# Second-phase weights: lower parts on GpSimd, w_k moved behind a gate, and the last products ordered by bank

## The chip, the cores and the metric

The kernel runs on one core of a Trainium2 chip. The metric is the device time in microseconds (us), the median of several runs, beside one execution that was profiled. Engines are named as in the profile: PE (TensorE, matmul), PEld (its weight load), DVE (VectorE), ACT (ScalarE), POOL (GpSimd), SP (SyncE, which here issues all DMAs).

## What is computed

```python
# attention between x (8 batches, 8 heads, 512 x 64) and a state of 32 rows a head
a   = softmax(x @ state.T / 8);  xread = a  @ state      # 512 rows
a2  = softmax(state @ x.T / 8);  sread = a2 @ x          # 32 rows
x   = concat([xread, sread])                             # 8 x 544 x 512
# first phase
h    = relu(x @ w_in)                                    # 512 -> 1024
conv = conv_w[0]*h[s-1] + conv_w[1]*h[s] + conv_w[2]*h[s+1]
y    = (h * sigmoid(conv)) @ w_out                       # 1024 -> 512
# second phase
prev = y shifted down by one row within a batch
xk = mu_k*y + (1-mu_k)*prev;  xr = mu_r*y + (1-mu_r)*prev
out = sigmoid(xr @ w_r) * (relu(xk @ w_k)**2 @ w_v)
```

Every fp32 operand of a large product is split in two: a high part that the PE's fast fp32 format (float32r) holds, and a low part, the operand less its high part. A product is then three matmuls: high x high, high x low, low x high.

## The kernel before

**Weights.** The weights come as 64-bit numbers. A `Weights` object loads two blocks of 128 x 512 at a time into a staging tile `raw` (line 143, on SP) and splits them: ScalarE makes a scaled copy in `mid` (L161) and converts in place (L163), VectorE puts the bits together in three steps (L164, L165, L166), ScalarE writes the high part (L168), and VectorE subtracts it for the low part (L169). `raw` and `mid` have two buffers each. The first phase uses the same two tags for the tiles `m` in `pair_m`. `weight()` returns the two functions, load and split; `weight_at(w, need, at)` hands both to the half slot `at` with the due number `500 * need - 1000`.

**First phase.** The work goes in slots (batch t, block f of 128 columns of d_ff; eight f a batch; t = 8 is a short one for the 32 state rows of all batches). In a slot `g1_main` makes `hps` on PE from the attention weights and M, the product of state and w_in; ScalarE evacuates it into `hb` (L452), a first tap on ScalarE (L468) and two on VectorE (L470) make the convolution, ScalarE takes the sigmoid (L478), VectorE multiplies (the gate, L479), ScalarE writes the high part of `gs` (L485), and the low part (L487) is made on GpSimd for batches 0 to 2 (`LOW_ON_POOL`), on VectorE later. Two slots on, `g1_sec` multiplies `gs` with w_out into four banks. GpSimd also sets the pads of `hb` (L451) and copies its ends into `carry` (L453). For each pair of batches, `pair_m` makes M in eight groups: ScalarE and VectorE evacuate it (L244, L245), and four DMAs a group copy it into place (L248).

**Second phase.** y goes through DRAM and comes back in nine tiles of tokens (384, seven times 512, 384). `mix` makes `xk` and `xr` for each of four column blocks c: ScalarE (L557), VectorE (L559), the high part on ScalarE (L564), the low part on VectorE (L565). `g2_main` multiplies with w_k, `g2_r` with w_r, and `g2_sec` multiplies the squared result `ks` with w_v into up to four banks; at the last f each bank is multiplied by the sigmoid (L616) and stored (L618).

**Order.** The program is written slot by slot; each piece carries a number (`tc.cur_priority`), and when the program is built a scheduler orders each engine's queue by these numbers and by what it takes to be ready. Space of the attention pool is given back at slot (7, 2), and from there the second phase's weights are announced. The queues run strictly in order. `behind(i)` (line 174) orders instructions traced inside it behind `i` where both are on the same engine's queue; it adds no semaphore.

## Time and profile before

| | |
|---|---|
| median of 3 runs | 883.36 us (883.15 to 884.06) |
| profiled execution | 881.77 us, its span 879.9 us |
| PE busy | 853.5 us, 97% of the span |
| PEld busy | 686.2 us, 78% |
| DVE busy | 546.4 us, 62% |
| ACT busy | 545.6 us, 62% |
| POOL busy | 105.4 us, 12% |

The span is what the trace shows of the profiled execution; the time of that execution is 1.9 us longer. Busy shares are means over the span; a stretch can look quite different. "Granted clock" is the share of full speed that the throttle gave TensorE. A row of the timeline begins with its start in us from the span's start and its duration in us.

### The profile page before, as it was taken

How to read it: one execution, taken by the hardware profiler on the slowest of the kernel's cores; microseconds unless marked ns; L12 is line 12 of the kernel's file. 1: busy time of each engine (PE TensorE's matmuls, PEld its weight loads, DVE VectorE, ACT ScalarE, POOL GpSimd, SP SyncE). 2: the span in 40 equal slices, each digit the busy share in tenths (PEclk: the TensorE clock that was granted, in tenths of full speed). 3: DMA queues.
4: the chain of work that ended last, by engine and by line, in shares of the span. 5: the costliest groups of instructions: out<-in, count | busy, mean ns of one | idle time of the engine just before them, and what ended most of it. 6: DMA issues, size and time to landing. Idle time of an engine off the chain costs nothing.

```text
span 879.9 us, 11844 instructions
## 1 busy us (share of the span) xinstructions
PE 853.5 (97%) x4406; PEld 686.2 (78%) x4406; DVE 546.4 (62%) x908; ACT 545.6 (62%) x952; POOL 105.4 (12%) x215
## 2 busy tenths in 40 slices
PE   5989999999999997999999999999999999999997
PEld 2557787788778775899888888888888888888886
DVE  6899987899799879999645533425334253332311
ACT  6787875787578658888756645636356364553421
POOL 1144543422111111210000000000000000000000
PEclk7899999999999998999999999999999999999999
DMA  9351254525534364233210211011100111001010
GB/s 340 116 197 49 102 143 128 150 75 160 156 114 121 96 197 151 96 144 120 98 48 37 49 48 31 17 48 49 48 23 26 49 48 48 19 18 48 1 48 36
DMA packets 45512, 76.85 MB, mean 87 GB/s; under 512 B 8336, under 2 KB 30352, under 8 KB 43408
## 3 DMA queue, kind: packets, MB, share of 16 engines
q1 hardware_dynamic: 45456, 76.12, 26.6%
q8 instruction: 34, 0.56, 0.3%
q14 instruction: 22, 0.18, 0.1%
HBM read 45.66 MB, written 17.86 MB: 72 GB/s over the span
## 4 chain that ended last, share of the span: by engine, by line
PE 88%; DVE 5%; ACT 3%; DMA 2%; SPq 1%; issue 1%; DVEq 0%; ACTq 0%
PE acc L115 14%; PE acc L116 14%; PE acc L117 14%; PE kps L115 7%; PE kps L116 7%; PE kps L117 7%; PE rps L117 4%; PE rps L116 4%; PE rps L115 4%; PE hps L115 3%; PE hps L117 3%; PE hps L116 3%; PE p_s L297 2%; PE p_m L116 1%; PE p_m L117 1%; SPq L248 1%
## 5 line engine op out<-in xcount | busy, mean ns | idle before, releaser
L594 DVE TENSOR_TENSOR ks<-k,ks 128x512 fp32r<-128x512 f32 (+1 forms) x72 | 47.6, 662 | 119.8 <-ACT ks L593 119.2
L116 PE MATMUL kps<-xk,k 128*128 128x512 f32 (+1 forms) x288 | 110.1, 382 | 0.0
L115 PE MATMUL kps<-xk,k 128*128 128x512 f32 (+1 forms) x288 | 110.1, 383 | 0.0
L117 PE MATMUL kps<-xk,k 128*128 128x512 f32 (+1 forms) x288 | 110.0, 382 | 0.0
L116 PE MATMUL acc<-gs,out 128*128 128x512 f32 (+1 forms) x288 | 109.6, 382 | 0.0
L117 PE MATMUL acc<-gs,out 128*128 128x512 f32 (+1 forms) x288 | 109.1, 380 | 0.0
L115 PE MATMUL acc<-v,ks 128*128 128x512 f32 x272 | 106.7, 392 | 0.0
L116 PE MATMUL acc<-v,ks 128*128 128x512 f32 x272 | 105.9, 389 | 0.0
L117 PE MATMUL acc<-v,ks 128*128 128x512 f32 x272 | 105.8, 392 | 0.0
L470 DVE SCALAR_TENSOR_TENSOR cacc<-hb,vcol,cacc 128x512 f32<-128x512 f32 (+1 forms) x138 | 103.3, 759 | 3.2 <-ACT cacc L468 2.7
L115 PE MATMUL acc<-gs,out 128*128 128x512 f32 (+1 forms) x288 | 95.0, 391 | 5.8 <-ACT gs L485 5.8
L559 DVE SCALAR_TENSOR_TENSOR mix<-yt,muc,mix 128x384 f32<-128x384 f32 (+7 forms) x128 | 61.4, 500 | 47.0 <-ACT mix L557 46.2
L593 ACT ACTIVATE ks<-k 128x512 fp32r<-128x512 f32 (+1 forms) x72 | 43.5, 605 | 71.2 <-PE acc L117 71.0
L557 ACT ACTIVATE mix<-yt,om 128x384 f32<-128x384 f32 (+7 forms) x128 | 61.5, 516 | 33.0 <-DMA yt<-y 16.2
L580 ACT ACTIVATE k<-kps 128x512 f32<-128x512 f32 (+1 forms) x72 | 40.9, 569 | 50.4 <-PE kps L117 50.0
L115 PEld LDWEIGHTS acc<-gs,out 128*128 128x128 f32 x288 | 54.0, 192 | 18.3 <-ACT gs L485 7.3
L116 PEld LDWEIGHTS acc<-gs,out 128*128 128x128 f32 x288 | 54.2, 188 | 13.1 <-issue 2.5
L565 DVE TENSOR_TENSOR xr<-mix,xr 128x512 fp32r<-128x512 f32 (+1 forms) x36 | 23.8, 661 | 62.8 <-ACT xr L564 62.8
L117 PEld LDWEIGHTS acc<-gs,out 128*128 128x128 f32 x288 | 54.2, 188 | 10.6 <-issue 0.8
L116 PEld LDWEIGHTS kps<-xk,k 128*128 128x128 f32 x288 | 54.4, 189 | 10.4
L117 PEld LDWEIGHTS kps<-xk,k 128*128 128x128 f32 x288 | 54.3, 188 | 10.2
L115 PEld LDWEIGHTS kps<-xk,k 128*128 128x128 f32 x288 | 54.2, 188 | 10.2
(138 smaller groups left out, 1762.1 us busy)
## 6 DMA issues: line engine op xcount, KB each, us to landing
out<-r SPq DMA_DIRECT2D x34, 256.0 KB, 2.0
xT<-x_t SPq DMA_DIRECT2D x32, 256.0 KB, 4.0
xn<-x_n SPq DMA_DIRECT2D x8, 1024.0 KB, 4.9
y<-yo SPq DMA_DIRECT2D x8, 1024.0 KB, 4.3
me<-m SPq DMA_DIRECT2D x48, 128.0 KB, 2.4
m_odd<-m SPq DMA_DIRECT2D x48, 128.0 KB, 2.4
raw<-w_out SPq DMA_DIRECT2D x8, 512.0 KB, 4.7
raw<-w_k SPq DMA_DIRECT2D x8, 512.0 KB, 4.5
```

The costliest lines, as they stand in the source:

```text
L115: nc.tensor.matmul(ps, lh, rh, start=start and k == 0, stop=False)
L116: nc.tensor.matmul(ps, lh, rl, start=False, stop=False)
L117: nc.tensor.matmul(ps, ll, rh, start=False, stop=stop and k == last)
L248: nc.sync.dma_start(out=m_of(b + j, q)[ri, :, g].bitcast(F32), in_=r[rj, :, i].bitcast(F32))
L297: nc.tensor.matmul(self.v["s", g][NS * j:NS * (j + 1), :], sT[self.b][r, h // 2, h % 2], xT[self.b][r, h // 2], start=True, stop=True,)
L470: nc.vector.scalar_tensor_tensor(a[:, :n], hb[:, k:k + n], w[k], a[:, :n], op0=ALU.mult, op1=ALU.add)
L557: nc.scalar.activation(tmp[:, o:o + m], y[:, c, q - 1:q - 1 + m], AF.Copy, scale=om[:, i:i + 1])
L559: nc.vector.scalar_tensor_tensor(tmp[:, o:o + m], y[:, c, q:q + m], muc[:, i:i + 1], tmp[:, o:o + m], op0=ALU.mult, op1=ALU.add,)
L565: nc.vector.tensor_tensor(dst[t][:, 1, c, :n], tmp[:, :n], hi.bitcast(F32), op=ALU.subtract)
L580: nc.scalar.activation(k[:, :n], s["p"][:, :n], AF.Relu)
L593: nc.scalar.activation(ks[:, 0, :n], s["k2"][:, :n], AF.Copy)
L594: nc.vector.tensor_tensor(ks[:, 1, :n], s["k2"][:, :n], ks[:, 0, :n].bitcast(F32), op=ALU.subtract)
```

## The change

The low parts of w_k, w_v and w_r are subtracted on GpSimd instead of VectorE (`helper=nc.gpsimd`). The low parts of the first second-phase tile's mixes, xk and xr, are too. The loads of w_k are ordered on SP behind the last copy of M; the ScalarE steps of w_k's splits are ordered behind the sigmoid of batch 7, f = 0, and their VectorE steps behind the gate of the same slot. In the last block of products with w_v, the three matmuls of each bank are ordered behind the last matmul of the bank before.

```diff
--- before.py
+++ after.py
@@ -1,4 +1,4 @@
-from contextlib import ExitStack
+from contextlib import ExitStack, nullcontext
 
 import concourse.bass as bass
 import concourse.tile as tile
@@ -14,6 +14,8 @@
 AX = mybir.AxisListType
 
 LOW_ON_POOL = (0, 1, 2)
+
+MIX_LOW_ON_POOL = (0,)
 
 CONV_ON_PE = 3
 
@@ -114,14 +116,16 @@
         for k, ((lh, ll), (rh, rl)) in enumerate(zip(lhs, rhs)):
             nc.tensor.matmul(ps, lh, rh, start=start and k == 0, stop=False)
             nc.tensor.matmul(ps, lh, rl, start=False, stop=False)
-            nc.tensor.matmul(ps, ll, rh, start=False, stop=stop and k == last)
+            end = nc.tensor.matmul(ps, ll, rh, start=False, stop=stop and k == last)
+        return end
 
 
     class Weights:
 
 
 
-        def __init__(self, src, many, n, pool, tag="", home=None):
+        def __init__(self, src, many, n, pool, tag="", home=None, helper=None):
+            self.helper = helper or nc.vector
             self.src, self.many, self.n, self.pool, self.tag, self.home = src, many, n, pool, tag, home
             self.wide = src[0].dtype != F32
 
@@ -166,7 +170,7 @@
             nc.vector.scalar_tensor_tensor(v, x, 3, v, op0=ALU.logical_shift_left, op1=ALU.bitwise_or)
             return (
                 nc.scalar.activation(hi, vf, AF.Copy),
-                nc.vector.tensor_tensor(lo, vf, hi.bitcast(F32), op=ALU.subtract),
+                self.helper.tensor_tensor(lo, vf, hi.bitcast(F32), op=ALU.subtract),
             )
 
     W = {}
@@ -175,10 +179,23 @@
 
         return tc.issue_after(i.ins)
 
-    def weight(src, key, tag, pool, k, many, group, home=None):
-
-
-        r = Weights([src[k + i] for i in range(many)], many, N, stg, home=home)
+    marks = {}
+
+    def after(fn, *keys):
+
+
+        def run():
+            with ExitStack() as stack:
+                for key in keys:
+                    stack.enter_context(behind(marks[key]))
+                fn()
+
+        return run
+
+    def weight(src, key, tag, pool, k, many, group, **how):
+
+
+        r = Weights([src[k + i] for i in range(many)], many, N, stg, **how)
 
         def split(first=0, n=many):
             g = (key, "group", k // group)
@@ -245,7 +262,9 @@
         nc.vector.tensor_tensor(r[:, 1], src, r[:, 0].bitcast(F32), op=ALU.subtract)
         for j, rj in HALF:
             for i, ri in HALF:
-                nc.sync.dma_start(out=m_of(b + j, q)[ri, :, g].bitcast(F32), in_=r[rj, :, i].bitcast(F32))
+                marks["m"] = nc.sync.dma_start(
+                    out=m_of(b + j, q)[ri, :, g].bitcast(F32), in_=r[rj, :, i].bitcast(F32)
+                )
 
     class Attention:
         def __init__(self, b, ap):
@@ -475,8 +494,8 @@
         n = width(t)
         s = st1[t, f]
         g = s["g"] = cp.tile([P, N], F32, tag="g", name="g")
-        nc.scalar.activation(g[:, :n], s["a"][:, :n], AF.Sigmoid)
-        nc.vector.tensor_tensor(g[:, :n], g[:, :n], s["hb"][:, 1:1 + n], op=ALU.mult)
+        marks["sigmoid", t, f] = nc.scalar.activation(g[:, :n], s["a"][:, :n], AF.Sigmoid)
+        marks["gate", t, f] = nc.vector.tensor_tensor(g[:, :n], g[:, :n], s["hb"][:, 1:1 + n], op=ALU.mult)
 
     def g1_c(t, f):
         n = width(t)
@@ -562,7 +581,8 @@
             )
         hi = dst[t][:, 0, c, :n]
         nc.scalar.activation(hi, tmp[:, :n], AF.Copy)
-        nc.vector.tensor_tensor(dst[t][:, 1, c, :n], tmp[:, :n], hi.bitcast(F32), op=ALU.subtract)
+        eng = nc.gpsimd if t in MIX_LOW_ON_POOL else nc.vector
+        eng.tensor_tensor(dst[t][:, 1, c, :n], tmp[:, :n], hi.bitcast(F32), op=ALU.subtract)
 
     def g2_main(t, f):
         n = W2[t]
@@ -610,7 +630,8 @@
         for i in range(W2[t] // P):
             sl = slice(i * P, (i + 1) * P)
             w = W["v", f]
-            mm3(ps[i], [(ks[:, 0, sl], ks[:, 1, sl])], [(w[:, 0], w[:, 1])], f == 0, f == KF - 1)
+            with behind(end) if i and (t, f) == (NT2 - 1, KF - 1) else nullcontext():
+                end = mm3(ps[i], [(ks[:, 0, sl], ks[:, 1, sl])], [(w[:, 0], w[:, 1])], f == 0, f == KF - 1)
             if f == KF - 1:
                 o = rt[t][:, i]
                 nc.vector.tensor_tensor(o, o, ps[i], op=ALU.mult)
@@ -754,15 +775,16 @@
                 ap_cm.__exit__(None, None, None)
                 p2 = ctx.enter_context(tc.tile_pool(name="p2", bufs=1))
                 for k in range(0, KF, 2):
-                    w = weight(w_k, "k", "wk", p2, k, 2, 2)
+                    w = weight(w_k, "k", "wk", p2, k, 2, 2, helper=nc.gpsimd)
+                    w = after(w[0], "m"), after(w[1], ("sigmoid", B - 1, 0), ("gate", B - 1, 0))
                     h = h2 + 2 * k
                     weight_at(w, h, h - 4)
                 for k in range(0, KF, 2):
-                    w = weight(w_v, "v", "wa", wp, k, 2, 4)
+                    w = weight(w_v, "v", "wa", wp, k, 2, 4, helper=nc.gpsimd)
                     h = h2 + 2 * k + 4
                     weight_at(w, h + 1, h - 3)
                 for k in range(0, KC, 2):
-                    w = weight(w_r, "r", "wb", wp, k, 2, 2)
+                    w = weight(w_r, "r", "wb", wp, k, 2, 2, helper=nc.gpsimd)
                     h = h2 + 8
                     weight_at(w, h, h - 2)
                 at_half(2 * i + 4, lambda: load_y(0, p2))
```

## Rows read from the trace of the kernel before

**Rows 1.** Waits of PE: what it waited for, us in total, times, longest us.

```profile
PE acc L115 <- ACT gs L485: 5.8, 2, 5.6
```

**Rows 2.** Busy time by stretch, six here and that of the twin passage.

```profile
core 0: us, PE busy (x) PEld busy (x) DVE busy (x) ACT busy (x) POOL busy (x), PEclk, DMA share, GB/s
320.00:330.40 10.40, 8.64 (x99) 6.14 (x97) 8.12 (x14) 7.79 (x12) 1.50 (x4) 1.00 0.78 208
...
330.40:335.90 5.50, 0.00 (x0) 0.00 (x0) 4.88 (x8) 5.49 (x8) 0.20 (x2) 0.81 0.99 373
335.90:340.70 4.80, 4.79 (x11) 3.79 (x12) 4.80 (x7) 4.80 (x8) 1.16 (x2) 0.51 0.01 3
...
336.00:417.00 81.00, 81.00 (x439) 72.02 (x440) 79.06 (x123) 69.19 (x121) 12.60 (x33) 0.97 0.30 108
417.00:447.00 30.00, 30.00 (x147) 26.05 (x146) 19.21 (x33) 21.49 (x43) 0.00 (x0) 1.00 0.23 80
...
238.60:249.00 10.40, 10.36 (x111) 7.25 (x110) 7.79 (x15) 9.97 (x17) 0.98 (x7) 1.00 0.69 203
```

**Rows 3.** Timeline of ScalarE at the passage from batch 6 to 7.

```profile
320.06 0.60 ACT L244 ACTIVATE m<-p_m 128x512 fp32r<-128x512 f32 x1 [2.28 <-PE p_m L117]
...
329.08 1.13 ACT L168 ACTIVATE k<-raw 128x1024 fp32r<-128x1024 f32 x1 [0.45 <-PE p_srT L396]
...
333.19 1.12 ACT L161 ACTIVATE mid<-raw 128x1024 f32<-128x1024 f32 x1
334.22 1.12 ACT L163 ACTIVATE raw<-raw 128x1024 uint32<-128x1024 uint32 x1
335.24 0.61 ACT L485 ACTIVATE gs<-g 128x512 fp32r<-128x512 f32 x1
```

**Rows 4.** Timeline of ScalarE at the passage from batch 4 to 5.

```profile
238.67 0.60 ACT L244 ACTIVATE m<-p_m 128x512 fp32r<-128x512 f32 x1 [2.71 <-PE p_m L117]
...
258.58 0.63 ACT L478 ACTIVATE g<-cacc 128x512 f32<-128x512 f32 x1 [0.96 <-DVE cacc L470]
```

**Rows 5.** Timeline of PE at the same passage: the first products with w_out.

```profile
248.13 1.07 PE L115 MATMUL acc<-gs,out 128*128 128x512 f32 x4
```

**Rows 6.** Timeline of the SP queue: four of the weights' loads.

```profile
309.13 1.40 SPq L143 DMA_DIRECT2D raw<-w_k  x2
...
326.69 0.97 SPq L143 DMA_DIRECT2D raw<-w_k  x2
...
360.60 0.80 SPq L143 DMA_DIRECT2D raw<-w_v  x2
384.72 1.94 SPq L143 DMA_DIRECT2D raw<-w_r  x4
```

**Rows 7.** The chain of waits at the end: start, us, what.

```profile
874.59 0.24 PE acc L117
...
874.85 0.69 DVE r L616
875.54 0.60 DVEq L847
876.14 0.60 DVE r L616
```

**Rows 8.** Timeline of VectorE: two gs lows, a weight low and a mix low.

```profile
308.46 1.17 DVE L487 TENSOR_TENSOR gs<-g,gs 128x512 fp32r<-128x512 f32 x1
...
313.53 0.69 DVE L487 TENSOR_TENSOR gs<-g,gs 128x512 fp32r<-128x512 f32 x1
...
343.29 1.21 DVE L169 TENSOR_TENSOR k<-raw,k 128x1024 fp32r<-128x1024 f32 x1
...
368.92 0.55 DVE L565 TENSOR_TENSOR xk<-mix,xk 128x384 fp32r<-128x384 f32 x1
```

**Rows 9.** Timeline of GpSimd: one subtract.

```profile
308.03 1.05 POOL L322 TENSOR_TENSOR q<-q,s 128x512 f32<-128x512 f32 x1 [4.22 <-DVE s L321]
```

**Rows 10.** GpSimd by line and shape: count, busy us, mean ns, idle before.

```profile
L487 POOL TENSOR_TENSOR gs<-g,gs 128x512 fp32r<-128x512 f32 x24 | 35.4, 1476 | 23.4 <-ACT gs L485 23.1
```

**Rows 11.** The conv taps (L470) on VectorE in two stretches: busy us and count.

```profile
100.00:130.00 30.00, 9.80 (x12) 1.00 0.41 112
...
280.00:300.00 20.00, 8.60 (x12) 1.00 0.39 113
```

## The prediction, as written before the result was known

> **What bounds the kernel now.** I read the waits of PE first, because PE is the busy engine: what is worth something is where it stands still. Only one wait of several us lies behind the start-up: 5.6 us before a product of the first phase that needs `gs`, the gated tile that ScalarE writes [rows 1]. Next, the busy time by stretch shows where this is and what the other engines do [rows 2]. From 320.0 to 330.4 PE works 8.64 of 10.4 us, from 330.4 to 335.9 not at all: 1.8 us in pieces and 5.5 in one, 7.3 us in all. The stretch behind it, 335.9 to 340.7, runs at a granted clock of 0.51, that is at 1.2 instead of 2.4 GHz: 4.8 x 0.49 = 2.4 us more. From 336 to 447 PE is never idle. So a change can gain in three places only: this gap, the slow clock behind it, and the end of the kernel. It can lose anywhere behind 336, and there the other columns matter: VectorE is busy 79.06 of 81 us from 336 to 417 and ScalarE 69.19, while 417 to 447 leaves VectorE 10.8 us free.
>
> **What fills the gap.** It lies at the passage from batch 6 to batch 7. ScalarE's queue tells the order of its work [rows 3]: between 329.08 and the `gs` at 335.24 that PE waits for stand a step of w_k's first split (L168, 1.13 us) and two steps of its second (L161 and L163, 1.12 us each), besides a table load and two sigmoids. The same passage from batch 4 to 5 has no second-phase weights in it and serves as a twin [rows 4, 5]: its last M evacuation is at 238.67, against 320.06 here, so the shift is 81.4 us. In the twin PE's product starts at 248.13, with PE busy 10.36 of 10.4 us from 238.6 [rows 2]. Shifted, it would start at 329.5, somewhat earlier even, since the last batch has no next scores to make. Here it starts at 335.9. The difference, 6.4 us or a little more, is most of the 7.3 us of idle time, found by another way.
>
> **Term 1, w_k behind the first gate.** All ScalarE and VectorE steps of the four w_k splits are put behind the sigmoid and the gate of batch 7, f = 0, in their own queues. No semaphore is waited for that was not before; it is an order of queues. At most the gap closes, 7.3 us; at least the three ScalarE steps in it go, 3.4 us. I take 6.8: the twin is the same code with the same queues, and half a microsecond of the pieces before 330.4 may stay, which w_k does not cause. The loads of w_k, eight DMAs in four pairs, are put on SP behind the last copy of M. Before, the first pair stood at 309.13, the second already behind the last copy at 326.69 [rows 6]. The first now goes out late, but the second pair, issued at 326.69, fed an L161 at 333.19, so a load needs at most 6.5 us, and the gate in question comes later than that: the twin's sigmoid of its f = 0 is at 258.58 [rows 4], shifted 340.0, a few us sooner without score work. Behind the loads on SP stand the load of the first y tile and of w_v, both needed tens of us later.
>
> **Term 2, the clock.** The 5.5 us without work are followed by the stretch at half clock. In 320.0 to 330.4, with 1.8 us of idle time in pieces, the granted clock stayed at 1.00 [rows 2]. If only such pieces remain, the 2.4 us come back whole; if 4 us remain in one piece, perhaps nothing does. I take 2.4.
>
> **Term 3, the last block bank by bank.** Before, the nine matmuls of the last f run with the six products of the high part first and the three closing ones last, so three banks close together and VectorE multiplies three times in a row, from 874.85 to 876.74 [rows 7]. Now a bank closes every third matmul: PE ends at the same time, two multiplies run beside it, and one of 0.69 us is left, done at 875.54. That is 1.2 us sooner, and the store behind it is the same. The low part that bank 0's closing product now needs sooner is made by VectorE while PE still works on the f before, so I charge no wait. Bounds 0.6 (one multiply saved) to 1.2.
>
> **Term 4, the lows on GpSimd and the splits moved into a full stretch.** Ten weight lows of 1.21 us and eight mix lows of 0.55 us leave VectorE [rows 8]: 16.5 us. GpSimd has no 1024-wide and no 384-wide subtract in this trace. The nearest rows are 512 wide: 1.05 us for one [rows 9] and 1.48 us on average for the 24 lows of the first batches [rows 10]. By width that gives, as an estimate, 2.1 to 3.0 us for a weight and 0.8 to 1.1 us for a mix, 27 to 38 us in all; up to 417 (seven of each) 20 to 29 us, where GpSimd did 12.6 us of work from 336 on [rows 2]. The two engines hinder each other: while GpSimd subtracted from 308.03 to 309.08, a VectorE subtract begun at 308.46 took 1.17 us; the next of that line took 0.69 [rows 8, 9]. The conv taps of L470 cost 9.80/12 = 0.82 us while the lows of batch 1 ran on GpSimd and 8.60/12 = 0.72 later [rows 11]. Such a slot holds two taps and a gate; with 0.1 us for each tap and somewhat more for the gate I charge 0.38 us of VectorE per low of 1.05 us, that is 36%, or about 10 us for 27. Relief is then 16.5 - 10 = 6.5 us net, between -10.5 us (16.5 against 27) and +16.5 us.
> What comes in: w_k's first split and a part of the second, which had used the gap, now have to fit into the full stretch up to 417. VectorE had 79.06 us of work there; the 81 us shrink to 78.6 with the clock back. Some 3.8 us of splits come in, seven lows of each kind go (12.3 us), and 36% of 20.3 us comes as hindrance (7.3 us): 77.9 us in 78.6. ScalarE goes from 69.2 to about 75. Both are full, so a part of the later splits slips, and there is room behind 417. By need, w_k's first pairs have tens of us in hand; its last pair, w_r and w_v have only a few, and each hands its staging buffer on 1 to 2 us later, since a GpSimd low is longer. Also queued behind a low on GpSimd are the pad memsets of `hb`, which may come 2 to 3 us late. I charge 1.5 us of new PE idle time, between 0 and 5.
>
> The Trainium skill (SBUF — State Buffer, section "Who interferes with whom") calls the port pair that VectorE and GpSimd share an exclusive lock: of a GpSimd instruction that reads SBUF and a VectorE instruction with two SBUF inputs, the one that comes second stands still for the whole of the other. The 1.17 us row agrees with it; the tap means show that VectorE is not caught each time. By the rule, the 16.5 us taken off VectorE could be paid back with 27 us, which is the lower end above and the third rival.
>
> **Sum.** 6.8 + 2.4 + 1.2 - 1.5 = 8.9 us. The profiled execution lasted 881.77 us (its span 879.9 and 1.9 us around it), the median of the runs is 883.36, 1.6 us more; the gain is put against the median: 874.5 us.
>
> **Rivals.**
> First, *another weight takes the place of w_k.* Only w_k is gated. If w_v's first pair took the free staging buffer at 309, its steps L161 to L166 would run in the same gap. Against it: buffers go out in the order of the code, not by due number: w_v's second pair (75,500) was loaded at 360.60, ahead of w_r (75,000) at 384.72 [rows 6]. Its price: only L168 and L169 leave the gap, some 2 us, the clock stays low, and the end gives 1.2: 883.4 - 3 = 880.
> Second, *the gain is given back before 447.* VectorE and ScalarE are so full that the PE time won is waited for at the start of the second phase, where w_k, w_r and the mixes have to be ready 9 us sooner. For it: 79.06 of 81 us. Against it: the room behind 417, and that the first batches had a GpSimd low in each slot and none of PE's long waits. With 9.5 of the 10.4 us given back: 882.5, no change.
> Third, *GpSimd locks VectorE out*, slower than before. If every low up to 417, at its contended length (7 x 3.0 + 7 x 1.1 = 28.7 us), stops VectorE for all of it, against 12.3 us taken off, VectorE has 16.4 us more to do in a stretch with 1.9 us free, and PE waits for some 14 us of it: 883.4 - 10.4 + 14 = 887. It decides from about 10 us of net loss. Against it: the 36% above.
> Fourth, the gap closes fully and nothing is lost behind it: 883.4 - 10.9 = 872.5.
>
> **Chances.** Forecast 0.68 (872.8 to 879), first rival 0.10, second 0.09, third 0.06, fourth 0.07. A measurement of this kernel tells about 0.2% (1.8 us) from no change. Faster: 0.68 + 0.10 + 0.07 = 0.85; within 0.2%: 0.09; slower: 0.06. The range 872.0 to 880.0 takes in the forecast, the fourth case and most of the first.
>
> **What would show it.** In the profile after: no PE wait of microseconds for `gs` near 330, and L161, L163 and L168 of w_k only behind the sigmoid of batch 7, f = 0 (term 1); a granted clock of 1.00 from 330 on (term 2); three multiplies at the end spaced by PE, not back to back (term 3); PE idle time, if any, between 385 and 445, and taps longer than 0.75 us there (term 4). I am wrong if another step fills the gap, or if PE's idle time behind 336 exceeds 5 us.

## The result and the profile after

The changed kernel takes 889.21 us (median of four executions, 889.01 to 891.04) against 883.71 us (883.15 to 884.40) for the kernel before beside it. The ratio is 1.0056, with an interval from 1.0036 to 1.0076: slower by 0.56%, 5.5 us, where 874.5 us had been forecast. The profiled execution of the changed kernel is its slowest, 891.04 us; that of the kernel before, 881.77 us, lies below all four of its executions here, so the two profiles lie further apart than the medians. Up to about 309 us the queues of both kernels hold the same instructions in the same order, and what differs there, some 4 us of PE idle time and clock between 150 and 240, is not of the change; the stretches behind 309 us are what is compared here.

The first lines of the page of the changed kernel give the busy time by engine. VectorE has 18 instructions fewer than before (890 against 908) and is busy 7.6 us longer (546.4 before); GpSimd is busy 37.1 us longer (105.4 before).

```profile
span 889.3 us, 11849 instructions
PE 855.0 (96%) x4406; PEld 685.9 (77%) x4406; DVE 554.0 (62%) x890; ACT 545.5 (61%) x952; POOL 142.5 (16%) x233
```

Next the busy time by stretch (start:end, length, then busy us of PE, PEld, DVE, ACT, POOL with instruction counts, granted clock, DMA share, GB/s), of the kernel before first, then of the changed one. It answers to [rows 2]. PE lost 7.27 us to idle time from 309 to 336 before; it loses 1.54 now, and the clock from 336 to 345 is 1.00 and not 0.74. Behind that PE was never idle before, though VectorE was busy for 58.72 of the 60 us from 345 to 405. Now PE is idle for 9.41 us there, while VectorE works 59.54 us, and the clock falls to 0.94 from 405 to 447.

```profile
309.00:336.00 27.00, 19.73 (x157) 15.69 (x155) 21.46 (x40) 18.73 (x29) 3.15 (x8) 0.96 0.76 243
336.00:345.00 9.00, 9.00 (x30) 7.24 (x31) 9.00 (x12) 8.97 (x14) 1.89 (x4) 0.74 0.01 3
345.00:405.00 60.00, 60.00 (x337) 53.27 (x337) 58.72 (x95) 49.05 (x89) 10.61 (x28) 1.00 0.33 123
```

```profile
309.00:336.00 27.00, 25.46 (x180) 20.27 (x179) 19.93 (x41) 17.63 (x30) 3.69 (x10) 1.00 0.49 151
336.00:345.00 9.00, 9.00 (x42) 7.44 (x40) 9.00 (x15) 7.98 (x12) 1.84 (x5) 1.00 0.43 165
345.00:405.00 60.00, 50.59 (x274) 42.45 (x273) 59.54 (x72) 45.23 (x79) 32.42 (x34) 0.99 0.32 111
405.00:447.00 42.00, 42.00 (x221) 39.26 (x222) 33.71 (x42) 32.14 (x58) 17.36 (x11) 0.94 0.38 131
```

The waits of PE from 336 to 447 name the tiles (what it waited for, us in total, times, longest). All belong to the first phase: `gs`, its low part, an `hb`, and `yo`, the copy of a result bank. No weight of the second phase is among them.

```profile
PE acc L117 <- ACT gs L504: 7.1, 2, 4.5
PE hps L117 <- ACT hb L477: 1.3, 1, 1.3
PE acc L118 <- DVE gs L506: 0.8, 1, 0.8
PE acc L117 <- DVE yo L523: 0.2, 1, 0.2
```

What VectorE and GpSimd do meanwhile is in their timelines (start, duration, line, operation). The first fence is VectorE, the second GpSimd, both of the changed kernel.

```profile
353.35 2.35 DVE L489 SCALAR_TENSOR_TENSOR cacc<-hb,vcol,cacc 128x512 f32<-128x512 f32 x1
356.23 2.31 DVE L489 SCALAR_TENSOR_TENSOR cacc<-hb,vcol,cacc 128x512 f32<-128x512 f32 x1
359.07 0.74 DVE L489 SCALAR_TENSOR_TENSOR cacc<-hb,vcol,cacc 128x512 f32<-128x512 f32 x1
...
400.40 2.65 DVE L489 SCALAR_TENSOR_TENSOR cacc<-hb,vcol,cacc 128x286 f32<-128x286 f32 x1
```

```profile
352.71 2.44 POOL L173 TENSOR_TENSOR k<-raw,k 128x1024 fp32r<-128x1024 f32 x1
...
355.15 2.84 POOL L173 TENSOR_TENSOR k<-raw,k 128x1024 fp32r<-128x1024 f32 x1
...
399.29 3.44 POOL L173 TENSOR_TENSOR v<-raw,v 128x1024 fp32r<-128x1024 f32 x1 [3.67 <-ACT v L172]
```

A tap takes 0.74 us; one that meets a weight low ends about half a us behind that low: the tap of 353.35 at 355.70, the low of 352.71 at 355.15. It goes the other way too: the low of 399.29 begins while VectorE runs a split step (399.26, 1.21 us), and takes 3.44 us. The last of these pairs makes the longest wait of PE, 4.47 us. The next two fences follow it on ScalarE and PE: the sigmoid waits 2.69 us for the tap of 400.40, the `gs` for the gate behind it, and PE 4.47 us for the `gs`. The chain begins with the low of w_v on GpSimd. The second-longest wait, 2.66 us at 363.96, ends differently: the gate of that tile was done at 360.41, but on ScalarE two steps of a w_v split stood ahead of its `gs`, the first of them waiting 0.75 us for its load, and the `gs` began at 363.30.

```profile
403.08 0.44 ACT L497 ACTIVATE g<-cacc 128x286 f32<-128x286 f32 x1 [2.69 <-DVE cacc L489]
404.30 0.44 ACT L504 ACTIVATE gs<-g 128x286 fp32r<-128x286 f32 x1 [0.78 <-DVE g L498]
```

```profile
404.80 1.27 PE L117 MATMUL acc<-gs,out 128*128 128x272 f32 x4 [4.47 <-ACT gs L504]
```

How much VectorE lost shows in its instructions by line and form from 300 to 447 us (busy us, mean ns of one). Of the kernel before first, then of the changed one; the same four forms, whose lines are L470, L479 and L166 before.

```profile
L470 DVE SCALAR_TENSOR_TENSOR cacc<-hb,vcol,cacc 128x512 f32<-128x512 f32 x26 | 19.0, 745 | 0.6 <-ACT cacc L468 0.6
L166 DVE SCALAR_TENSOR_TENSOR raw<-mid,raw 128x1024 uint32<-128x1024 uint32 x10 | 12.2, 1222 | 0.1
L470 DVE SCALAR_TENSOR_TENSOR cacc<-hb,vcol,cacc 128x286 f32<-128x286 f32 x16 | 8.2, 511 | 0.0
L479 DVE TENSOR_TENSOR g<-g,hb 128x286 f32<-128x286 f32 x8 | 3.6, 451 | 0.0
```

```profile
L489 DVE SCALAR_TENSOR_TENSOR cacc<-hb,vcol,cacc 128x512 f32<-128x512 f32 x27 | 23.8, 891 | 0.7 <-ACT cacc L487 0.7
L170 DVE SCALAR_TENSOR_TENSOR raw<-mid,raw 128x1024 uint32<-128x1024 uint32 x10 | 14.4, 1435 | 0.1
L489 DVE SCALAR_TENSOR_TENSOR cacc<-hb,vcol,cacc 128x286 f32<-128x286 f32 x16 | 12.4, 777 | 0.1
L498 DVE TENSOR_TENSOR g<-g,hb 128x286 f32<-128x286 f32 x8 | 6.7, 833 | 0.0
```

And GpSimd's, of the changed kernel: a weight low takes 2.5 to 2.8 us, a mix low 1.4. The 18 lows are 37.9 us.

```profile
L173 POOL TENSOR_TENSOR v<-raw,v 128x1024 fp32r<-128x1024 f32 x4 | 11.1, 2764 | 15.3 <-ACT v L172 15.3
L173 POOL TENSOR_TENSOR k<-raw,k 128x1024 fp32r<-128x1024 f32 x4 | 10.8, 2707 | 0.4 <-ACT k L172 0.4
L585 POOL TENSOR_TENSOR xk<-mix,xk 128x384 fp32r<-128x384 f32 x4 | 5.5, 1376 | 3.5 <-ACT xk L583 3.5
L585 POOL TENSOR_TENSOR xr<-mix,xr 128x384 fp32r<-128x384 f32 x4 | 5.4, 1362 | 0.5 <-ACT xr L583 0.5
L173 POOL TENSOR_TENSOR r<-raw,r 128x1024 fp32r<-128x1024 f32 x2 | 5.1, 2534 | 9.1 <-ACT r L172 9.1
```

The 18 subtracts had been 16.5 us of VectorE. It is busy 7.6 us longer without them, so the rest of its work grew by 24.1 us: 64% of the lows' 37.9 us on GpSimd. The totals of kernels without these lows on GpSimd (before, e1, e4, e16) differ by 1.3 us.

Two of the change's parts did what they were to do. On ScalarE, from M's last evacuation (324.11) w_k's first step waits until 342.05, behind the first sigmoids of batch 7, where before three of w_k's steps stood between 329 and the `gs` that PE waited for [rows 3], and two more ahead of them:

```profile
324.11 0.60 ACT L261 ACTIVATE m<-p_m 128x512 fp32r<-128x512 f32 x1 [2.28 <-PE p_m L119]
...
333.77 0.62 ACT L504 ACTIVATE gs<-g 128x512 fp32r<-128x512 f32 x1
...
342.05 1.14 ACT L165 ACTIVATE mid<-raw 128x1024 f32<-128x1024 f32 x1
```

At the end, the last of the three multiplies is over at 886.27 (one row for three instructions), 0.73 us behind PE's last matmul, which ends at 885.54; before it was 876.73 behind 875.27, 1.46 us [rows 7].

```profile
884.22 2.05 DVE L637 TENSOR_TENSOR r<-r,acc 128x512 f32<-128x512 f32 x3 [3.58 <-PE acc L119]
```

```profile
885.15 0.39 PE L119 MATMUL acc<-v,ks 128*128 128x512 f32 x1
```

### The profile page after: what moved, and what is told of

It reads as the page before. It is cut to its first block, busy times and chain, and to the rows that moved or that the text cites. A ratio compares the mean times of both kernels' runs of the same rounds, so it can differ in the third digit from the quotient of the medians.

```text
span 889.3 us, 11849 instructions
## 1 busy us (share of the span) xinstructions
PE 855.0 (96%) x4406; PEld 685.9 (77%) x4406; DVE 554.0 (62%) x890; ACT 545.5 (61%) x952; POOL 142.5 (16%) x233
## 4 chain that ended last, share of the span: by engine, by line
PE 80%; DVE 11%; ACT 4%; DMA 2%; issue 2%; SPq 1%; ACTq 0%; DVEq 0%
PE acc L117 12%; PE acc L119 12%; PE acc L118 12%; PE kps L117 7%; PE kps L118 7%; PE kps L119 7%; PE rps L119 3%; PE rps L118 3%; PE rps L117 3%; DVE cacc L489 3%; PE hps L117 2%; PE hps L119 2%; PE hps L118 2%; PE p_s L316 2%; DMA me<-m 1%
## 5 line engine op out<-in xcount | busy, mean ns | idle before, releaser
L489 DVE SCALAR_TENSOR_TENSOR cacc<-hb,vcol,cacc 128x512 f32<-128x512 f32 (+1 forms) x138 | 112.3, 824 | 3.4 <-ACT cacc L487 2.7
L578 DVE SCALAR_TENSOR_TENSOR mix<-yt,muc,mix 128x384 f32<-128x384 f32 (+7 forms) x128 | 64.2, 522 | 51.2 <-ACT mix L576 50.2
L118 PEld LDWEIGHTS kps<-xk,k 128*128 128x128 f32 x288 | 54.9, 191 | 10.3
L117 PEld LDWEIGHTS kps<-xk,k 128*128 128x128 f32 x288 | 54.7, 190 | 10.3 <-ACT xk L583 0.2
L119 PEld LDWEIGHTS acc<-gs,out 128*128 128x128 f32 x288 | 54.3, 189 | 10.5 <-issue 0.8
L497 ACT ACTIVATE g<-cacc 128x512 f32<-128x512 f32 (+1 forms) x69 | 41.8, 606 | 30.2 <-DVE cacc L489 19.0
```

Of the source, the lines that this page charges most:

```text
L117: nc.tensor.matmul(ps, lh, rh, start=start and k == 0, stop=False)
L118: nc.tensor.matmul(ps, lh, rl, start=False, stop=False)
L119: end = nc.tensor.matmul(ps, ll, rh, start=False, stop=stop and k == last)
L489: nc.vector.scalar_tensor_tensor(a[:, :n], hb[:, k:k + n], w[k], a[:, :n], op0=ALU.mult, op1=ALU.add)
L497: marks["sigmoid", t, f] = nc.scalar.activation(g[:, :n], s["a"][:, :n], AF.Sigmoid)
L578: nc.vector.scalar_tensor_tensor(tmp[:, o:o + m], y[:, c, q:q + m], muc[:, i:i + 1], tmp[:, o:o + m], op0=ALU.mult, op1=ALU.add,)
```

## The experiments

Two theories stood after the result. **L, the lows**: GpSimd and VectorE stop each other, and that costs more VectorE time than the moved subtracts had been. **F, the full stretch**: from 345 to 405 VectorE has no free time even without that, so what the passage wins is waited for behind it. Two further theories come up in the expectations: **S**, that the chain of the ten splits, which pass through two staging buffers, begins too late; and **Q**, that a split's step holds up ScalarE's queue. All kernels are built from the changed one, and the code cuts are abridged; differences are given against the kernel before in the same session, whose median lay between 883.6 and 884.5 us. Single executions of one kernel differ by 2 to 7 us; in the profiles, waits of PE for the copies of M differ by some us ahead of 309.

### e1, all lows back on VectorE

```diff
-    w = weight(w_k, ..., helper=nc.gpsimd)      # w_v and w_r too
+    w = weight(w_k, ...)
-MIX_LOW_ON_POOL = (0,)
+MIX_LOW_ON_POOL = ()
```

> The change without its GpSimd part: all lows stay on VectorE, w_k behind the gate and the bank order stay. Theory L (the GpSimd lows lock VectorE out of SBUF and that is the whole loss): the gap at the passage 6 to 7 is closed as in the changed kernel, nothing is lost behind it, 873 to 877 us. Rival F (VectorE and ScalarE are too full for the splits once the gap is closed, whoever makes the lows): PE waits of several us between 350 and 420 stay, and VectorE has 16 us more own work, 886 to 893 us.

Measured: 883.49 us (882.02 to 885.53, 12 executions) against 884.38; ratio 0.9983 (0.9968 to 0.9997). It lies between the two expectations, and neither theory alone is right. The lows on GpSimd cost the difference to the changed kernel, some 6 us, but without them the gain of the passage isn't there either. The windows of this kernel show where it went: 309 to 336 is as good as in the changed kernel (1.11 us idle), 336 to 345 runs at 1.00, and PE is idle 5.24 us from 345 to 405, at a clock of 0.97.

```profile
309.00:336.00 27.00, 25.89 (x182) 20.61 (x181) 20.37 (x41) 18.14 (x30) 4.05 (x10) 1.00 0.52 161
336.00:345.00 9.00, 9.00 (x41) 7.48 (x40) 9.00 (x15) 8.35 (x12) 1.49 (x4) 1.00 0.34 132
345.00:405.00 60.00, 54.76 (x296) 47.24 (x296) 59.41 (x92) 50.88 (x88) 18.74 (x26) 0.97 0.34 125
```

The longest of these waits, 2.68 us, shows what stands in the way. The first fence is ScalarE, the second PE. A step of a w_r split waits 1.94 us for its load and the split's next step follows; behind both stands a sigmoid whose last tap had ended at 391.69 at the latest. The gate behind that sigmoid then waits until 395.06 for another step of the split on VectorE. So here it is first ScalarE's queue and then VectorE's.

```profile
391.70 1.16 ACT L165 ACTIVATE mid<-raw 128x1024 f32<-128x1024 f32 x1 [1.94 <-DMA raw<-w_r]
392.76 1.12 ACT L167 ACTIVATE raw<-raw 128x1024 uint32<-128x1024 uint32 x1
393.79 0.42 ACT L497 ACTIVATE g<-cacc 128x286 f32<-128x286 f32 x1
```

```profile
396.10 0.78 PE L117 MATMUL acc<-gs,out 128*128 128x272 f32 x4 [2.68 <-ACT gs L504]
```

### e2, the lows on GpSimd alone

```diff
-    w = after(w[0], "m"), after(w[1], ("sigmoid", B - 1, 0), ("gate", B - 1, 0))
-    with behind(end) if i and (t, f) == (NT2 - 1, KF - 1) else nullcontext():
+    with nullcontext():
```

> The GpSimd part alone: lows of w_k, w_v, w_r and of the first mixes on GpSimd, no gate for w_k, no bank order. Theory L: VectorE instructions of 2 to 3 us appear beside the lows and PE waits between 340 and 420: 8 to 13 us slower than before, 892 to 897 us. Rival F: VectorE is relieved and nothing is squeezed, so 881 to 884 us.

Measured: 894.12 us (893.06 to 897.27, 6); ratio 1.0119 (1.0099 to 1.014), +9.7 us, as theory L expected. The subtracts cost VectorE more on GpSimd than at home (551.2 us busy against 546.4), and this by itself is more than the whole loss of the change.

### e4, the order by bank alone

```diff
-MIX_LOW_ON_POOL = (0,)
+MIX_LOW_ON_POOL = ()
-    helper=nc.gpsimd              # three times
-    w = after(...)                # w_k's loads and splits
```

> The bank order of the last block alone. All theories: the last three multiplies are spaced by PE and the last one ends 1.2 us sooner after PE's last matmul, so 0.6 to 1.2 us less than before, 882.5 to 883.1 us.

Measured: 883.20 us (881.05 to 885.48, 12); ratio 0.9987 (0.9974 to 1.0), -1.2 us with an interval from -2.3 to 0. The traces give the better figure: VectorE ends 0.72 us behind PE in this kernel and 0.73 in the changed one, against 1.46 before.

### e7 and e8, which lows

e7 has the weight lows on GpSimd and the mix lows on VectorE, e8 the reverse.

```diff
-MIX_LOW_ON_POOL = (0,)
+MIX_LOW_ON_POOL = ()         # e7
-    helper=nc.gpsimd          # e8, three times
```

> The changed kernel with the mix lows back on VectorE; only the weight lows are on GpSimd. Theory L: the weights hold some 27 of the 38 us of GpSimd lows, so most of the loss against all lows on VectorE (5.7 us) stays: 886 to 889 us. If the mixes, whose four steps share one buffer, are what hurts: 883 to 885 us.

> The changed kernel with the weight lows back on VectorE; only the first tile's mix lows are on GpSimd. Theory L: 884 to 886 us, against 883.5 with all lows on VectorE. If the mixes are what hurts: 887 to 890 us.

Measured: e7 888.60 us (887.09 to 890.67, 5), ratio 1.0061 (1.0038 to 1.0084); e8 883.96 us (882.22 to 887.05, 10), ratio 1.0002 (0.9987 to 1.0018). The weight lows carry nearly all of it: e7 is within 1 us of the changed kernel, e8 within 1 us of e1.

### e5, each weight low in four pieces

```diff
-    self.helper.tensor_tensor(lo, vf, hi.bitcast(F32), op=ALU.subtract)
+    for j in range(0, self.n, P):
+        s = slice(j, j + P)
+        i = self.helper.tensor_tensor(lo[:, :, s], vf[:, :, s], hi[:, :, s], op=ALU.subtract)
```

> The changed kernel with each weight low cut into four subtracts of 256 columns on GpSimd. Theory L, by sums: VectorE is stopped for 0.5 to 0.9 us at a time instead of 2 to 3, but the port is held as long in all, so 886 to 892 us. Rival S (it is the single long stops that hit the gate and tap chains): VectorE slips in between, 880 to 885 us.

Measured: 889.26 us (888.33 to 890.07, 5); ratio 1.0065 (1.0043 to 1.0086), the time of the changed kernel. So shorter stops brought no time. The 40 pieces of 1.02 to 1.11 us are 41 us on GpSimd, where the ten lows were 27; with the mix lows it is 53 us. VectorE's other work grew by 20.3 us, somewhat less than the 24.1 of the changed kernel, so the sum of VectorE's loss doesn't explain why the time is the same.

The growth per us of lows on GpSimd differs between the kernels: 64% in the changed one, 61% in e2 and e7, 38% here, 32% in e8. GpSimd's own time may be part of the reason, since it grows where VectorE stops it: a mix low takes 2.1 us on the mean in e8 and 1.4 in the changed kernel.

### e6, the lows without their reads

```diff
-    self.helper.tensor_tensor(lo, vf, hi.bitcast(F32), op=ALU.subtract)
+    for j in range(2):
+        self.helper.memset(lo.bitcast(F32), 0.0)
+    self.helper.tensor_tensor(lo[:, :, :1], vf[:, :, :1], hi[:, :, :1], op=ALU.subtract)
+    ...                                           # the mixes' lows likewise
```

> The changed kernel, but each GpSimd low is two fills of the same width and a subtract of one column a block, so GpSimd is busy about as long and hands the tile on as late, yet reads almost nothing; the low parts of these weights and mixes are left out of the result. Theory L (what VectorE loses is the port that GpSimd's reads hold): VectorE's instructions beside them are back at 0.6 to 0.75 us, it is truly relieved of 16 us, and 874 to 880 us result. Rival G (GpSimd is simply slow, so weights, mixes and buffers come late): 887 to 891 us as in the changed kernel.

Measured: 884.75 us (880.43 to 887.29, 10) against 883.99; ratio 0.9999 (0.9977 to 1.0021). It lies between the expectations, and far below the changed kernel: with two fills (2.0 us a weight) in place of each subtract (2.5 to 2.8 us), the 512-wide taps are back at 747 ns, the short ones at 509. The low parts are missing from this kernel's result. One form got longer, the split's `tensor_scalar` with one input (L169; line 176 of this kernel): 994 ns on the mean of ten against 692 before, nearly all in one instance. It lay beside a run of fills from 364.46 to 368.08, and a copy of two columns on GpSimd ended with it.

```profile
365.04 3.58 DVE L176 TENSOR_SCALAR mid<-mid 128x1024 f32<-128x1024 f32 x1
```

So the reads are what VectorE's two-input work meets, and this one step with one input stood still while GpSimd did little but write; PE waited 2.38 us for a low part of `gs` soon after, at 371.07. The fills wait for no result of ScalarE, unlike the subtracts, so the tiles are also handed on sooner here; it is the taps' rows, more than the time, that speak for the reads. The Trainium skill (SBUF — State Buffer, section "Who interferes with whom") says both: a two-input VectorE instruction contends with GpSimd instructions that read SBUF and not with those that only write, and a VectorE instruction in a two-port mode, which `tensor_scalar` can enter, contends with GpSimd, with no such limit to reads. These rows agree, though none names the mode of the step.

### e10 and e12, other places for single splits

Both are e1 with one thing moved. In e10 w_k's first pair is not gated; in e12 w_r's pairs come behind w_k's last.

```diff
+    if k:                                                   # e10
         w = after(w[0], "m"), after(w[1], ("sigmoid", B - 1, 0), ("gate", B - 1, 0))
-    weight_at(w, h, h - 2)                                  # e12
+    weight_at(w, h + 3, h)
```

> The changed kernel with all lows on VectorE, and only the second to fourth pair of w_k behind the first gate; the first pair is loaded and split as before, in the passage's early part. It stands against the kernel with all four pairs gated and the lows on VectorE (883.5). Theory S, what takes the passage's gain back is the late begin of the chain of splits (two staging buffers, ten splits one after the other): the chain begins one pair sooner, and some 4 us of the 8 won stay: 878 to 881. Theory F, it is VectorE, which has no free time from 345 to 405: one split (L168 to L173, about 4 us of VectorE) leaves that stretch and is paid in the passage, where VectorE has some 5 us free in 320 to 345 but its queue then holds back the gs of the passage: 881 to 884, with PE waiting near 330 again.

> The changed kernel with all lows on VectorE, and the two pairs of w_r loaded and split behind the last pair of w_k instead of ahead of it. It stands against 883.5. Theory S: the same ten splits run through the same two buffers, but what ScalarE waits for near 390 (2.6 us in all, a w_r load) is no longer w_r; if the chain's length decides, nothing moves: 882.5 to 884.5; if it was the place of w_r's split ahead of the gated tiles of the last slot of the first phase, the wait near 396 goes, 880 to 882. Theory F: VectorE has the same work in the same stretch: 883 to 885.

Measured: e10 882.85 us (881.33 to 888.21, 11) against 883.61, ratio 0.9999 (0.9982 to 1.0015); e12 883.27 us (881.5 to 885.09, 11), ratio 0.999 (0.9977 to 1.0003). Neither moves the time; theory S had put e10 at 878 to 881. e10 is the plainest picture of a trade: from 345 to 385 PE is never idle, but from 330.4 to 345 it is idle 3.5 us at a clock down to 0.81. One split more in the passage, one less behind it, and the lost time is the same.

### e11, one tap less in batch 7

e1 without one of batch 7's two VectorE taps, 6.1 us less on VectorE in the stretch. The convolution of batch 7 is incomplete in it.

```diff
-    for k in (1, 2):
+    for k in (1, 2)[:1 + (t != B - 1)]:
```

> The changed kernel with all lows on VectorE and one of the two VectorE taps of the convolution of batch 7 left out (so this part of the result is not computed): eight instructions of about 0.76 us, 6.1 us, leave VectorE between 340 and 395, and nothing else changes, the staging of the weights least of all. It stands against 883.5. Theory F, VectorE's full stretch gives the gain back: most of these 6 us come off the end, 877 to 880, and PE's idle time from 345 to 405 shrinks by half or more. Theory S, the chain of staging does: 882 to 884, with the waits of PE near 396 for gs still there.

Measured: 878.68 us (878.07 to 879.75, 5); ratio 0.9946 (0.9933 to 0.9958), -4.9 us, 4 us more than e1 at the middle. This is what theory F expected: relief of VectorE in this stretch comes off the end, two thirds of it. In its windows PE is idle 2.94 us from 345 to 405, at a clock of 1.00, against 5.24 at 0.97 in e1; that is a little less than the half that F had expected. A tap less also makes each tile's way to its gate shorter by about 0.75 us, and this run doesn't tell the two apart.

```profile
345.00:405.00 60.00, 57.06 (x325) 50.05 (x324) 58.02 (x90) 52.28 (x91) 11.40 (x25) 1.00 0.42 155
```

### e13 and e14, the work for r behind the first phase

e13 takes the w_r splits and the mixes for r behind the sixth gate of t = 8, with e12's order; e14 is the same without w_k's gate.

```diff
+    w = w[0], after(w[1], ("sigmoid", B, 5), ("gate", B, 5))            # w_r
-    at_half(h2 + 2 + c, lambda c=c: mix(0, 1, c, p2))
+    at_half(h2 + 2 + c, after(lambda c=c: mix(0, 1, c, p2), ("sigmoid", B, 5), ("gate", B, 5)))
-    if f >= 4 and f - 4 < W2[t] // P:
+    f0 = 4 if t else 5
+    if f >= f0 and f - f0 < W2[t] // P:
```

> All lows on VectorE, w_k behind the first gate and the bank order kept; and what the first phase doesn't need is moved out of VectorE's full stretch: the two w_r splits go behind the last w_k split and behind the sixth gate of the last slot of the first phase, the four mixes for r behind that gate too, and the r products of the first tile one position later. In the kernel without this (883.5) these were 6.2 us of split steps and 2.3 us of mixes on VectorE between 392 and 405, where PE lost 2.7 us to a wait and 1.8 to the clock; the last w_k split takes a part of the room. Theory F (VectorE's full stretch takes the gain back): the wait near 396 and the slow clock go, 878.5 to 881. Theory S (the chain of the splits): the chain is as long as before and its last members start later, PE waits behind 405 instead, 883 to 887.

> The same, with w_k not put behind the first gate. Theory F: the gap at the passage is back with its slow clock (9.7 us of PE), and VectorE has no PE wait behind it to give, so the move of w_r is worth nothing here: 882 to 884.5; the difference to the kernel with the gate, 2 to 5 us, is what the gate is worth once VectorE has room. Theory S: 882 to 884 too, but with no difference between the two.

Measured: e13 884.97 us (882.69 to 886.5, 12) against 884.51, ratio 0.9998 (0.9985 to 1.0011); e14 884.12 us (881.48 to 888.15, 12), ratio 0.9992 (0.9978 to 1.0006). Theory F had expected 878.5 to 881 for e13, and 2 to 5 us between the two, and neither came. Theory S had expected no difference between them, and 884.97 lies in its range for e13, though the wait of PE did not move behind 405 as S had it. The trace says what stood in the way. VectorE now has time to spare from 385 to 405 (18.40 of 20 us busy), and PE still waits near 396. The three fences are SP, ScalarE and PE of e13: w_k's last pair has taken w_r's place in the chain of splits. Its load goes out when the staging buffer comes free, at 386.17; ScalarE stands 2.89 us at the split's first step; two sigmoids are queued behind it; and PE waits 2.99 us for the `gs` that follows them.

```profile
386.17 0.80 SPq L147 DMA_DIRECT2D raw<-w_k  x2
```

```profile
391.30 1.15 ACT L165 ACTIVATE mid<-raw 128x1024 f32<-128x1024 f32 x1 [2.89 <-DMA raw<-w_k]
```

```profile
395.69 1.00 PE L117 MATMUL acc<-gs,out 128*128 128x272 f32 x4 [2.99 <-ACT gs L504]
```

It is the picture of e1 again, with w_k in place of w_r. So F needs a second half, theory Q: a split's first step, waiting for its load, holds up ScalarE's queue.

### e16, e17, e15 and e18, splits kept apart

e16 is e1 with w_r's two splits behind the fourth and sixth gate of t = 8; e17 is e1 with w_k's second and fourth pair behind the third gate of batch 7 instead of the first; e15 has both, and e18 is e15 again.

```diff
+    w = w[0], after(w[1], ("sigmoid", B, 3 + k), ("gate", B, 3 + k))                           # w_r: e16, e15
-    w = after(w[0], "m"), after(w[1], ("sigmoid", B - 1, 0), ("gate", B - 1, 0))
+    w = after(w[0], "m"), after(w[1], ("sigmoid", B - 1, k % 4), ("gate", B - 1, k % 4))       # w_k: e17, e15
```

> All lows on VectorE, w_k behind the first gate, bank order; and only the place of the w_r splits is changed: the first pair behind the fourth gate of the last slot of the first phase, the second behind the sixth. With w_k's last pair in that place (883.5 to 885) ScalarE stood 2.9 us at the split's first step, waiting for its load, with the sigmoids of two finished tiles queued behind it, and PE waited 3.0 us for the gs of the first. Theory Q, this wait is one of order in ScalarE's queue: with the sigmoids ahead of the step the wait near 396 goes, and its slow clock with it, 4.5 us: 879 to 881. Theory F, VectorE would not have been there sooner anyway: 882.5 to 884.5, with a PE wait of 2 to 3 us for the same gs.

> The same, and the second and fourth pair of w_k behind the third gate of batch 7 in place of the first, so that the first two splits don't run in a row. In the kernel without it PE waits 0.8 us for an evacuation and 0.95 for a gs between 353 and 361, where the two splits run close together. Theory Q: these go, 1 to 1.8 us less than with the w_r order alone, 877.5 to 880. Theory F: VectorE is full whichever way its work is ordered, and the waits only move on: no difference to the kernel with the w_r order alone, within 1 us.

> All lows on VectorE, w_k behind the gates, bank order; the first and third pair of w_k behind the first gate of batch 7, the second and fourth behind the third, and w_r where the changed kernel has it. Against the same with all four pairs behind the first gate (883.5) and with w_r held back as well (880.7). Theory Q, what helps is that two splits no longer run in a row between 341 and 356: 880 to 882, and w_r's place (which alone moved nothing) is worth under 1 us. Theory F: VectorE is full whichever way, the waits move on, and the 880.7 was a chance of the runs: 882.5 to 884.

> The kernel with w_k spread and w_r held back a second time (880.7 the first time, over executions from 879.7 to 883.0, of which the profiled one was the slowest). Theory Q: 880 to 881.5 again, and PE idle for 3 to 4 us between 345 and 447 in a profile of a middling run. Theory F: 882.5 to 884, idle for 4.5 us or more there.

Measured, against 884.34 and 884.07 us before: e16 883.29 us (881.59 to 888.12, 12), ratio 0.9995 (0.9977 to 1.0013); e17 883.6 us (881.36 to 885.94, 11), ratio 0.999 (0.9976 to 1.0004); e15 880.69 us (879.66 to 883.01, 6), ratio 0.9951 (0.9934 to 0.9968); e18 881.63 us (879.12 to 883.92, 9), ratio 0.9968 (0.9953 to 0.9983). Either move alone does nothing that can be told, as theory F expected. e16 is no fair test of Q, though: PE still waits 2.56 us there, for a `gs` whose gate was done at 390.30, and the `gs` began only at 392.40, behind the first two steps of a split on ScalarE. They wait for no load now but are still ahead of it. Both moves together give 2.4 to 3.7 us, and this version beats both kernels by a little; e18 lies just above the range that theory Q gave it. In a profile of e18 PE's idle time from 345 to 405 is still 4.59 us, where theory Q had expected 3 to 4 from 345 to 447, but in shorter waits, and the clock stays at 1.00:

```profile
345.00:405.00 60.00, 55.41 (x317) 49.04 (x316) 59.39 (x92) 50.61 (x86) 16.24 (x26) 1.00 0.36 134
```

Its longest wait is 2.39 us for a `gs`; e1's is 2.68 and the changed kernel's 4.47. Why the two moves help together and neither alone is not shown: the stretch's idle time differs by under 1 us between the profiles of e1, e15, e16, e17 and e18 (4.6 to 5.3 us), and each is one execution.

### The lost PE time beside the measured time

For a few kernels, what the windows say of one execution each: PE's idle time from 309 to 447, and behind it the time that the granted clock took (one less the clock, by the length of the windows behind 336; it counts idle time too, so it is somewhat high).

| kernel | idle, us | clock, us | both, less that of before | measured, less before |
|---|---|---|---|---|
| before | 7.3 | 2.3 | | |
| changed | 11.0 | 3.1 | +4.5 | +5.5 |
| e2, lows alone | 13.9 | 5.2 | +9.5 | +9.7 |
| e7, weight lows | 8.3 | 5.5 | +4.2 | +4.6 |
| e8, mix lows | 7.5 | 1.8 | -0.3 | 0.0 |
| e1, no lows | 6.4 | 1.8 | -1.5 | -0.9 |
| e11, one tap less | 4.0 | 0 | -5.6 | -4.9 |
| e18, splits apart | 5.7 | 0 | -4.0 | -2.4 |

The last two columns agree within 1.6 us (the 0.7 us at the end is in neither window), so the change is decided in this stretch. Of the kernels left out, e10 and e12 to e17 agree within 1.7 us, and e4 within 2.5 (+1.3 against -1.2). Two kernels don't fit: e5 and e6, with 11.5 and 5.4 us lost here, would be at +1.9 and -4.2 and were measured at +5.3 and +0.8. Why is open; each profile is one execution.

## Why the prediction was wrong

**Term 1, right in place and about right in size.** The gap at the passage closed: 7.27 us of idle time became 1.54, 5.7 where I had put 6.8 and bounds of 3.4 and 7.3. What stays are waits for the copies of M, not steps of w_k. The shifted twin was a good guide: PE's product of the first `gs` came 10.3 us behind M's last evacuation, 9.5 in the twin and 15.9 before.

**Term 2, right in its place.** The clock is 1.00 from 330 to 345, and the 2.3 us are back. Behind the new waits it falls again, to 0.79 from 405 to 417, and the table puts that loss at 3.1 us.

**Term 3, right in kind, too large.** 0.73 us in the trace, for 1.2 with bounds of 0.6 and 1.2, and close to the lower one. I had the last multiply at its lone duration of 0.69 us right behind PE's end, and took PE's end from the first of the three back-to-back multiplies, 874.85; PE itself ended at 875.27.

**Term 4 is the step that failed, in two places.** The first is a size. I charged 36% of the lows' time as hindrance, from taps beside 512-wide lows of the first batches. Measured it is 64%: 24.1 us for 37.9. The total of the lows was at the upper end of my estimate (38 us), so the hindrance was 24.1 where I had 10, and the net relief not 6.5 us but -7.6. It lies inside the bounds that I gave (-10.5 to +16.5; the lower one goes by 27 us of lows, and by 38 it would be -21.5). That VectorE stands still beside these lows is shown: with the reads, +9.7 us (e2); without them, the taps are normal (e6); without the lows on GpSimd, the loss is gone (e1). Why the share is 64% and not 36% is not settled. The taps came from 100 to 130 us, where work with both inputs in SBUF was 19.3 of 30 us on VectorE, and from 345 to 405 it is all but 6.2 of 60, so a low meets it more often; but in the same later stretch e5 shows 38% and e8 32%.

The second is a way of counting. I set 77.9 us of VectorE work against 78.6 us of room and called it fitting, with 1.5 us of new PE idle time. It was 9.41 us, and without any of these lows on GpSimd (e1) it is still 5.24 us, with 1.8 lost to the clock: 7.0 of the 8.5 us that the passage won in e1 (6.2 of idle time, 2.3 of clock). A sum of busy time leaves out the order: the splits that came into the stretch stand in the strict queues ahead of the gated tiles, and each tile behind them comes late. The gap of the passage and the waits behind it are two ends of one shortage: e10 moves one split from the one side to the other and the time stays, e11 takes work away and the time falls. The busy share alone doesn't say it, for VectorE was nearly as full before (58.72 of 60 us against 59.41 in e1) and PE never waited there. Whether VectorE's time or the split steps in ScalarE's queue count for more is open: in e1 and in the changed kernel, waits of 2.7 us go back to ScalarE's queue in part.

The sign that the prediction named for being wrong, more than 5 us of PE idle time behind 336, came.

**The rivals.** The second, gain given back because VectorE and ScalarE are full, is the outcome that e1 shows: 883.5 against my 882.5. What is late is not what I named, though. It is not w_k, w_r and the mixes at the start of the second phase but the `gs` of batch 7 and of t = 8, still in the first. The third, the lock, is what the change adds to it: I put its point at about 10 us of net loss on VectorE, and 7.6 us were enough, for by e1 the second had already used up the gain; it gave 887 by my working, and 889.2 came. They are not alternatives but stand on each other, and giving them 0.09 and 0.06 apart was the error of the chances. The first rival didn't come: w_v's first load went out at 355.18, behind w_k's first two pairs.

**The measure of the wrongness.** As differences to the kernel before, -8.9 us had been forecast. With 1.1 less from term 1 and 0.5 less from term 3 it would be -7.3, and +5.5 came. Term 4 stands for the 12.8 us between: 6.4 for the waits behind the passage (e1 came at -0.9) and 6.4 for the lows on GpSimd (+5.5 against -0.9).

## What to carry to other kernels

Moving a two-input subtract from VectorE to GpSimd took its time off VectorE and gave more back here, because VectorE was running two-input work at the same time. Count the GpSimd time that it will take, and charge VectorE a share of it measured in the same stretch; it was 61 to 64% in the three kernels with whole weight lows on GpSimd, and 32 and 38% in the other two. Before closing a gap ahead of a stretch in which another engine is busy nearly all the time, ask what the work moved into that stretch will stand ahead of: here 7.0 of 8.5 us came back as waits, whatever the due numbers said. And a step that waits for a load delays everything behind it in its queue, so behind the work that is ready is the place to try for it; e16 alone, which took the load's wait away and left the steps ahead of the tile, gained nothing.

## What the runs showed of the hardware

- GpSimd copies of two columns took 0.60 us on the mean from 300 to 447 before and 0.81 in the changed kernel. Two of them, begun at 347.39, lasted 5.36 us together, while VectorE ran two-input steps back to back, split steps of 1.23 us among them. The weight low queued behind them on GpSimd began when they ended, at 352.71.
- Weight lows in four pieces gave the time of whole ones (e5: 889.26 us, against 889.21), with 41 us on GpSimd in place of 27 and 20.3 us more of VectorE's other work in place of 24.1.
- Fills on GpSimd, which read nothing, left two-input VectorE work alone (taps of 747 and 509 ns, 745 and 511 before), but beside them a one-input fp32 `tensor_scalar` took 3.58 us in place of 0.69 (e6).
